# Zero products, one product piece per unit and other spacing in the forward loop of a training-step kernel

## The chip, the cores and the metric

The kernel runs on one core of a Trainium2 chip. The metric is the time of one execution on the device in microseconds (us): the median of seven runs, with the lowest and the highest. Beside these there is one execution taken with the hardware profiler. Its own time is given too, because all durations below come from it.

A core has five engines that run side by side: TensorE (PE: matmuls, and PEld: their weight loads), VectorE (DVE), ScalarE (ACT), GpSimd (POOL) and SyncE (SP, which here only issues DMAs). TensorE writes its results into PSUM, which has eight banks of 128 x 512 float32.

## The reference

It is one transformer block with adaptive layer norm, forward and backward, on 2048 tokens of width 512. There are 32 attention heads of 16 columns and a hidden layer of 1792. Weights and activations are bfloat16.

```python
sa, ca, ga, sb, cb, gb = split(silu(c) @ w_mod, 6)
h = layernorm(x) * (1 + ca) + sa
q, k, v = heads(h @ wqkv)
x = x + ga * (softmax(q @ k.T * 16 ** -0.5) @ v) @ wo
h = layernorm(x) * (1 + cb) + sb
z = relu(h @ w1 + b1)
x = x + gb * ((z * z) @ w2 + b2)
# returned: x and the gradients of x, wqkv, wo, w1, b1, w2, b2, c and w_mod for grad_out
```

## The kernel before, in words

The kernel has three parts: a preparation, a forward loop, and everything after it (the last dense chunk, the backward pass of the attention, the last products). The change is in the forward loop. It also adds one memset to the preparation.

The forward loop has 512 units (`NF`): four chunks of 512 queries, in each chunk eight groups of four heads, in each group 16 tiles of 128 keys (`TT`). A unit `u` does this, and the order in which it is written here is the order on each engine, since the whole loop is built with a manual schedule:

- `run_due`: DMAs and other small jobs that an earlier unit put off with `later(lag, ...)`.
- In units with `u % 16 == 4` (10 in the first seven groups), `fload`: nine DMAs on SP for the heads that come twelve or more units later.
- `fscore(u)`: four score matmuls in two pairs. A pair is 32 rows by 128 columns of the array each, side by side in different row strips, into one tile `psST` of two banks; there are three such tiles. ScalarE takes the exponential of a pair from `psST` to `ET` (line 555).
- `fpv(u - 2)`: four matmuls of 128 rows by 32 columns, side by side in column strips, add exponentials times values to the bank `oacc` (line 569). After the 16th key tile, which is in the units with `u % 16 == 1`, VectorE copies `oacc` to `ostage` (line 573). There is one `oacc` bank, so the next group's first `fpv` waits for this copy.
- The planned products of the preparation in units 0 to 100 (`plan`): projections, norms, and transposes `ptk` (line 1056).
- `step(u)`: one step of the dense work, described next. In units 101 to 143, and at other times, there is none.

The six `psST` banks and the `oacc` bank leave one bank for all products: the tile `pm`, which `mm()` gives out with one buffer. A product waits until VectorE has read the one before it from `pm`.

The dense work for a query chunk is a generator, `dense_chunk`. It is begun when that chunk's attention is done: chunk 0 near unit 136, chunk 1 near 264, chunk 2 near 392. Chunk 3 is done after the loop. `step` resumes the generator once for each unit, and what it yields is the number of units to wait. A yield of -2 makes `step` run a weight-gradient chain in the same unit (`next_chain`: four matmuls on line 228, and a copy of the result on line 246). Ripe chains also take units of their own. The stages are, in order:

- four pieces with `wo` (line 342), each followed on VectorE by a copy, two elementwise operations and a layer-norm statistic (lines 343, 324, 325, 329, 330);
- 14 products with `w1` (line 393);
- 14 products `dz` with the transposed `w2` (line 407). After every third one, chains are forced until few enough stand in the queue `dwq`, and then the result goes to `to_tokens`, which transposes it by a DMA and queues new chains;
- four `dx` products of 14 matmuls each (line 429), spread over four units, with a layer-norm gradient on VectorE (`finish_dx`, lines 456 to 461). The last `finish_dx` is run when the generator is resumed after the last product;
- four products with `w2` (line 480) from the weight tile `wB`, which SP loads in seven slices, and four with the transposed `wo` (line 512).

`open_group[0]` tells that a product which is spread over several units still holds the `pm` bank.

Of the kernel before, what the change touches and what calls it, by code (L numbers as in the profile page):

```python
# [17 lines left out]
BF = dt.bfloat16  # L18
# [16 lines left out]
def kernel(  # L35
# [29 lines left out]
    masks.make_identity(nc, identf[:])  # L65
    ones_bf = persist.tile([P, P], BF, name="ones_bf")
    DVE.memset(ones_bf[:], 1.0)
    onesf = persist.tile([P, 4], F32, name="onesf")
    DVE.memset(onesf[:], 1.0)
    modbc = persist.tile([P, 6, D], BF, name="modbc")  # L70
# [74 lines left out]
    with ExitStack() as ph:  # L145
# [6 lines left out]
        racc = ffw.tile([P, 5, D], F32, name="racc")  # L152
        pools = {}

        def mm():
            return pools["mm"].tile([P, 512], F32, name="pm", tag="pm")

        def flat(x):
# [156 lines left out]
        def dense_chunk(c, O_c, L):  # L315
# [23 lines left out]
            for ti in range(4):  # L339
                pa = mm()  # L340
                for oc in range(DC):
                    PE.matmul(pa[:], OT[:, ti, oc, :], L["wo"][:, oc, :], start=(oc == 0), stop=(oc == DC - 1))
                DVE.tensor_copy(a_c[:, ti, :], pa[:])
                with_input(ti)
                stats(ti)
                yield 0
            woT = ffw.tile([P, DC, D], BF, name="woT", tag="wo")
            later(3, sp, woT[:], woT_st[:])
            h2T = cb.tile([P, 4, DC, P], BF, name="h2T", tag="T4")
# [54 lines left out]
            for fc in range(FC):  # L404
                pds = mm()
                for oc in range(DC):
                    PE.matmul(pds[:], w2T[:, oc, fc * P:(fc + 1) * P], gfT[:, :, oc, :],
                              start=(oc == 0), stop=(oc == DC - 1))
                db1p = wk.tile([P, 1], F32, name="db1p", tag="db1p")
                DVE.scalar_tensor_tensor(out=dzT[:, fc, :], in0=pds[:], scalar=2.0, in1=rT[:, fc, :],  # L410
                                         op0=ALU.mult, op1=ALU.mult, accum_out=db1p[:])
                POOL.tensor_tensor(db1acc[:, fc:fc + 1], db1acc[:, fc:fc + 1], db1p[:], ALU.add)
                if fc % 3 == 2 or fc == FC - 1:
                    f0 = fc // 3 * 3
                    while len(dwq) > FC - (fc + 1) + n_dz[0]:
                        yield -2
                    to_tokens("dz", dzT, f0, fc + 1)
                yield 0
            if c == QC - 2:
                begun["w1"] = load_wA(w1_src, 1)  # L420
            yield 1
# [3 lines left out]
            for ti in range(4):  # L425
                t = 4 * c + ti
                pdh = mm()
                for fc in range(FC):
                    PE.matmul(pdh[:], dzT[:, fc, ti * P:(ti + 1) * P], w1T[:, fc, :],
                              start=(fc == 0), stop=(fc == FC - 1))  # L430
                    if fc == 3 and rest:
                        rest.pop()()
                    if fc % 4 == 3:
                        open_group[0] = True
                        yield 0
                open_group[0] = False
                xn2 = xn2_c[:, ti, :]
                dxn2 = wk.tile([P, D], BF, name="dxn2", tag="dxn2")
                s1 = wk.tile([P, 1], F32, name="s1b", tag="s1b")
                DVE.tensor_tensor_reduce(out=dxn2[:], in0=pdh[:], in1=cb1_bc, scale=1.0, scalar=0.0,  # L440
                                         op0=ALU.mult, op1=ALU.add, accum_out=s1[:])
                prod2 = wk.tile([P, D], BF, name="prod2", tag="tc")
                s2 = wk.tile([P, 1], F32, name="s2b", tag="s2b")
                DVE.tensor_tensor_reduce(out=prod2[:], in0=dxn2[:], in1=xn2, scale=1.0, scalar=0.0,
                                         op0=ALU.mult, op1=ALU.add, accum_out=s2[:])
                rowsum(1, dxn2[:], t)
                rowsum(2, prod2[:], t)
                c12 = wk.tile([P, 2], F32, name="c12", tag="c12")
                DVE.tensor_scalar(c12[:, 0:1], s1[:], 1.0 / D, None, ALU.mult)
                DVE.tensor_scalar(c12[:, 1:2], s2[:], 1.0 / D, None, ALU.mult)  # L450
                tq = wk.tile([P, D], BF, name="tqb", tag="ta")
                DVE.tensor_scalar(tq[:], xn2, c12[:, 1:2], c12[:, 0:1], ALU.mult, ALU.add)

                def finish_dx(ti=ti, t=t, dxn2=dxn2, tq=tq):
                    uq = wk.tile([P, D], BF, name="uqb", tag="tb")
                    DVE.tensor_tensor(uq[:], dxn2[:], tq[:], ALU.subtract)
                    DVE.scalar_tensor_tensor(out=dx1_c[:, ti, :], in0=uq[:], scalar=rstd2[:, t:t + 1], in1=g_c[:, ti, :],
                                             op0=ALU.mult, op1=ALU.add)
                    proda = wk.tile([P, D], BF, name="proda", tag="tc")
                    DVE.tensor_tensor(proda[:], dx1_c[:, ti, :], a_c[:, ti, :], ALU.mult)  # L460
                    DVE.tensor_tensor(da_c[:, ti, :], dx1_c[:, ti, :], ga_bc, ALU.mult)
                    rowsum(3, proda[:], t)

                rest.append(finish_dx)
                yield 0
            rest.pop()()
            chains = [add_chain(c, 3, FC + 4 * NS + a, D, lambda ti, a=a: O_c[:, ti, a * P:(a + 1) * P], lambda ti: da_c[:, ti, :],
# [89 lines left out]
        def fpv(u):  # L557
            qc, hg, kt = funits[u]
            if kt == 0:
                fcur["o"] = pools["o"].tile([P, 512], F32, name="oacc", tag="oacc")  # L560
                if hg == 0:
                    fcur["rr"] = ework.tile([H, 512], F32, name="rrows", tag="rrows", bufs=1)
                    fcur["ou"] = ework.tile([P, 4, HG, P], BF, name="O_un", tag="O_un", bufs=1)
            oacc = fcur["o"]
            ET = fe.pop(u)
            for hq in range(4):
                h = hg * 4 + hq
                lhsT = vaug[:, kt].rearrange("p h c -> p (h c)")[:, h * (DH + 1):h * (DH + 1) + 32]
                PE.matmul(oacc[32 * hq:32 * hq + 32, :], lhsT, ET[:, hq, :],  # L569
                          start=(kt == 0), stop=(kt == TT - 1), tile_position=(0, 32 * hq), skip_group_check=True)  # L570
            if kt == TT - 1:
                ostage = ework.tile([P, 512], F32, name="ostage", tag="ostage", bufs=1)
                DVE.tensor_copy(ostage[:], oacc[:])  # L573
                obf = ework.tile([P, 512], BF, name="obf", tag="obf", bufs=2)
                if u == NF - 1:
                    fcur["last"] = ostage
                    return
                if hg == HG - 1:
                    DVE.tensor_copy(obf[:], ostage[:])
                else:  # L580
                    POOL.tensor_copy(obf[:], ostage[:])
                for hq in range(4):
                    h = hg * 4 + hq
                    later(2, sp, fcur["rr"][h:h + 1, :], ostage[32 * hq + 16:32 * hq + 17, :])
                later(3, sp, fcur["ou"][:, :, hg, :], obf[:], True)
                if hg == HG - 1:
                    fdone.append((u + 7, qc, fcur["rr"], fcur["ou"]))

        def scale_heads(O_c, ou, ti, t, g):
            DVE.tensor_tensor(O_c[:, ti, 0:64 * g].rearrange("p (g h d) -> p g h d", g=g, h=4),  # L590
# [111 lines left out]
        def turn_weights(i):  # L702
            if i == 2:
                turned["1"] = ffw.tile([P, FC, D], BF, name="w1T_0", tag="wB")
                turned["2"] = ffw.tile([P, DC, FF], BF, name="w2T_0", tag="wA")
                turned["o"] = ffw.tile([P, DC, D], BF, name="woT_0", tag="wo")
            if 2 <= i < 6:
                for fc in range(4 * (i - 2), min(FC, 4 * (i - 2) + 4)):
                    sp(turned["1"][:, fc, :], B_w1[:, fc * P:(fc + 1) * P], True)
            if 7 <= i < 11:  # L710
                sp(turned["2"][:, i - 7, :], B_w2[:, (i - 7) * P:(i - 6) * P], True)
                sp(turned["o"][:, i - 7, :], A_wo[:, (i - 7) * P:(i - 6) * P], True)
            if i == 12:
                sp(w1T_st[:], turned["1"][:])
                sp(w2T_st[:], turned["2"][:])
                sp(woT_st[:], turned["o"][:])
# [421 lines left out]
        with ExitStack() as ph2:  # L1138
# [3 lines left out]
            with tc.manual_schedule(engines={PE.engine, ACT.engine, DVE.engine, SP.engine, POOL.engine}):  # L1142
                fh[0, 0] = (qts[0], kts[0])
                for u in range(NF + 2):
# [9 lines left out]
                        later_stage(stages[u // 4])  # L1154
                    if u % 4 == 0 and 18 <= u // 4 < 32:
                        turn_weights(u // 4 - 18)
                    for f, args in plan.pop(u, ()):
                        f(*args)
                    if u < NF - 4:
                        step(u)  # L1160
                    elif dwq and u >= NF - 2:
                        next_chain()
                    if u >= NF - 7 and "L" in loads and "O" not in loads["L"]:
                        early_finish()
                    if u == NF:
# [853 lines left out]
```

## Time and profile before

| | |
|---|---|
| seven runs | median 2582.5 us, 2578.74 to 2585.96 |
| the profiled execution | 2594.22 us, span 2592.2 us |
| mean granted TensorE clock | 0.910 |
| the forward loop in it | about 41 to 1037 us |
| behind the loop | 1037 to 2592.2 us |
| PE / DVE / ACT / POOL busy over the span | 91% / 70% / 89% / 13% |

In the page's groups, a row gives line, engine, operation, what it writes and reads, the count, the busy time, the mean of one in ns, and the idle time of the engine just before these instructions with what ended it. In tables by stretch, a row is a stretch (from:to in us from the start of the span), then the busy time of each engine with its number of instructions, the granted TensorE clock (1.00 is full speed) and the share of the DMA engines. In a timeline, a row is the start, the duration, the engine, the line and the operation, how many were merged, and in brackets the engine's idle time before the row with what ended it. Matmuls overlap in the pipeline and their ends are modelled, so a busy PE is not PE at its peak.

### The profile page before, as it was taken

The numbers are of one execution on the slowest core, as the hardware profiler recorded it, in microseconds if no ns is written. First come the engines' busy times: TensorE is split into PE (matmuls) and PEld (weight loads), VectorE is DVE, ScalarE is ACT, GpSimd is POOL, SyncE is SP. The second block draws the span as 40 slices with busy tenths as digits, with TensorE's granted clock in tenths as the row PEclk, the third lists the DMA queues.
The fourth block names the chain that finished last, engine by engine and source line by source line (L and its number), as shares of the span: only waits on it lengthen the run. The fifth ranks groups of instructions, "written<-read, shape, count | busy, mean of one in ns | idle before, by whom it ended". The sixth has DMA issues, their size and how long they took to land.

```text
span 2592.2 us, 49491 instructions
## 1 busy us (share of the span) xinstructions
PE 2355.8 (91%) x18468; PEld 761.3 (29%) x18468; DVE 1812.9 (70%) x2316; ACT 2312.3 (89%) x3577; POOL 348.1 (13%) x370
## 2 busy tenths in 40 slices
PE   7888999889988989999999999999899999999999
PEld 3232123222322322432222222222222222222243
DVE  5555253454444444578999989899898998999862
ACT  7999999999989999539999999999999999999943
POOL 2000101211323132210101101011010110100100
PEclk9995589989988999998999989999998998999999
DMA  6476563357548656979999999999999999999972
GB/s 202 127 195 170 145 154 95 90 156 152 81 94 179 124 118 126 259 214 187 198 189 198 188 197 196 190 194 191 196 196 195 205 195 195 196 197 207 191 240 76
DMA packets 1227126, 447.15 MB, mean 172 GB/s; under 512 B 1103095, under 2 KB 1197751, under 8 KB 1226630
## 3 DMA queue, kind: packets, MB, share of 16 engines
q1 hardware_dynamic: 1198966, 409.14, 79.6%
q0 software_dynamic: 10944, 16.78, 4.6%
q10 hardware_dynamic: 16976, 18.07, 2.5%
q8 instruction: 145, 2.38, 0.4%
q14 instruction: 95, 0.78, 0.1%
HBM read 96.75 MB, written 73.95 MB: 66 GB/s over the span
## 4 chain that ended last, share of the span: by engine, by line
PE 48%; ACT 34%; DVE 7%; issue 6%; DMA 2%; SPq 1%; ACTq 0%; POOL 0%; DVEq 0%; POOLq 0%
ACT E_u L1585 20%; ACT ET L555 9%; PE dqacc L1657 6%; PE psST L553 5%; PE psS_A L1579 4%; PE accVK L1630 3%; ACT dsT L1728 3%; PE oacc L569 3%; PE psS_C L1579 3%; PE pm L228 3%; PE psS_B L1579 2%; PE pm L393 2%; PE accVK L1639 2%; PE pdh L1843 2%; PE pwq L1877 2%
## 5 line engine op out<-in xcount | busy, mean ns | idle before, releaser
L1599 DVE TENSOR_TENSOR dS_u<-psD_u,E_u 128x1024 bf16<-128x1024 f32 x1024 | 1187.5, 1220 | 115.6 <-PE psS_B L1579 69.0
L555 ACT ACTIVATE ET<-psST 128x1024 bf16<-128x1024 f32 x1024 | 945.9, 1190 | 54.1 <-PE psST L553 53.5
L1585 ACT ACTIVATE E_u<-psS_A 128x512 bf16<-128x512 f32 x768 | 507.3, 661 | 26.7 <-PE psS_B L1579 9.6
L1585 ACT ACTIVATE E_u<-psS_B 128x512 bf16<-128x512 f32 x768 | 503.6, 656 | 6.2 <-PE ptT L1620 2.3
L1597 PE MATMUL psD_u<-iv,ido 32*128 32x512 bf16 x2048 | 429.7, 403 | 0.2
L553 PE MATMUL psST<-qt_sb,kt_sb 32*128 32x512 bf16 x2048 | 353.0, 431 | 55.3 <-ACT ET L555 42.7
L1585 ACT ACTIVATE E_u<-psS_C 128x512 bf16<-128x512 f32 x512 | 334.2, 653 | 1.1 <-PE accVK L1639 0.7
L1579 PE MATMUL psS_B<-ik,iq 32*128 32x512 bf16 x768 | 311.5, 406 | 12.7 <-ACT E_u L1585 5.2
L1579 PE MATMUL psS_A<-ik,iq 32*128 32x512 bf16 x768 | 309.7, 403 | 12.7 <-ACT E_u L1585 1.3
L569 PE MATMUL oacc<-ET,vaug 128*32 128x512 bf16 x2048 | 230.6, 440 | 7.0 <-DVE ostage L573 7.0
L1630 PE MATMUL accVK<-dS_u,qz 128*32 128x512 bf16 x2048 | 230.1, 418 | 0.3 <-DVE dS_u L1599 0.2
L1579 PE MATMUL psS_C<-ik,iq 32*128 32x512 bf16 x512 | 194.9, 381 | 33.0 <-ACT dsT L1728 29.0
L1579 PEld LDWEIGHTS <-iq 32*128 32x128 bf16 x2048 | 129.1, 92 | 313.7 <-issue 298.5
L1639 PE MATMUL accVK<-E_u,dOs_tok 128*16 128x512 bf16 x2048 | 208.7, 397 | 0.0
L1675 POOL TENSOR_TENSOR dQacc<-dQacc,dqtmp 128x512 f32<-128x512 f32 x64 | 81.2, 1268 | 885.3 <-ACT dqtmp L1670 885.3
L1657 PE MATMUL dqacc<-dsT,KS_tok 128*32 128x512 bf16 x2048 | 189.6, 482 | 11.2 <-DMA dsT<-dS_u 2.2
L553 PEld LDWEIGHTS <-kt_sb 32*128 32x128 bf16 x2048 | 87.2, 93 | 345.8 <-issue 327.5
L246 DVE COPY part<-pm 128x512 f32<-128x512 f32 (+2 forms) x103 | 63.5, 617 | 134.9 <-PE pm L228 132.5
L1728 ACT ACTIVATE dsT<-ptT 128x1024 bf16<-128x1024 bf16 x128 | 149.0, 1164 | 2.9 <-PE ptT L1620 2.7
L1597 PEld LDWEIGHTS <-ido 32*128 32x128 bf16 x2048 | 107.3, 91 | 109.1 <-issue 105.3
L1630 PEld LDWEIGHTS <-qz 128*32 128x32 bf16 x2048 | 61.4, 99 | 243.4 <-issue 230.8
L1620 PE MATMUL ptT<-identb,dS_u 128*128 128x128 bf16 x1024 | 79.2, 221 | 33.0 <-ACT dsT L1728 26.3
(400 smaller groups left out, 2309.8 us busy)
## 6 DMA issues: line engine op xcount, KB each, us to landing
p_st<-part POOLq DMA_DIRECT2D x36, 256.0 KB, 5.4
kt_sb<-qkT_st SPq DMA_DIRECT2D x124, 64.0 KB
wA<-in_B_w_dram SPq DMA_DIRECT2D x28, 256.0 KB
dsT<-dS_u SPq DMA_TRANSPOSE x448
wB<-w1T_st SPq DMA_DIRECT2D x21, 256.0 KB
wA<-w2T_st SPq DMA_DIRECT2D x21, 256.0 KB
wB<-in_B_w_dram SPq DMA_DIRECT2D x21, 256.0 KB
p_st<-part POOLq DMA_DIRECT2D x25, 192.0 KB, 4.3
```

The lines of the kernel that those rows point to most:

```text
L553: PE.matmul(ps[:, hi, :], kt_sb[r:r + 32, kt * P:(kt + 1) * P], qt_sb[r:r + 32, :], start=True, stop=True, tile_position=(r, 0))
L555: ACT.activation(ET[:, 2 * pair:2 * pair + 2, :], ps[:], AF.Exp, scale=SCALE)
L569: PE.matmul(oacc[32 * hq:32 * hq + 32, :], lhsT, ET[:, hq, :], start=(kt == 0), stop=(kt == TT - 1), tile_position=(0, 32 * hq), skip_grou ...
L1579: PE.matmul(psS[:], st["q"][r:r + 32, qt * P:(qt + 1) * P], st["k"][r:r + 32, kc * 512:kc * 512 + 512], start=True, stop=True, tile_positi ...
L1585: ACT.activation(bst[u][0][:, hq, :], sst.pop((u, hq))[:], AF.Exp, scale=SCALE)
L1597: PE.matmul(psD[:, hi, :], st["do"][r:r + 32, qt * P:(qt + 1) * P], st["v"][r:r + 32, kc * 512:kc * 512 + 512], start=True, stop=True, til ...
L1599: DVE.tensor_tensor(dS_u[:, 2 * pair:2 * pair + 2, :], psD[:], E_u[:, 2 * pair:2 * pair + 2, :], ALU.mult)
L1630: PE.matmul(cur["vk"][32 * hq:32 * hq + 32, :], hst[hg]["qz"][:, qt, hq, :], bst[u][1][:, hq, :], start=(qt == 0), stop=False, tile_positi ...
L1639: PE.matmul(acc[32 * hq:32 * hq + DH, :], dOs_tok[:, qt, (hg * 4 + hq) * DH:(hg * 4 + hq + 1) * DH], E_u[:, hq, :], start=False, stop=(qt ...
L1657: PE.matmul(acc[32 * hq:32 * hq + 32, :], KS_tok[:, kc * 4 + kt, h * DH:h * DH + 32], tT[:, :, hq * 4 + kt, :], start=(kt == 0), stop=(kt ...
L1675: POOL.tensor_tensor(dst2, dst, tmp[:], ALU.add)
L1728: ACT.activation(dst, pt[:], AF.Identity)
```

## The change

It has four parts, all in the forward loop.

- A tile of zeros, 128 x 16, is set once. `steady(u - 2)` adds two matmuls with these zeros as weights to `oacc`, so the values there stay what they are. It is called at the end of a unit in which `mm()` was not called and no spread product holds `pm`, and not in a unit whose `fpv` was the 16th key tile. This is the case in 133 units.
- In the `dz` stage, the `yield 0` after each product stands before the forced chains and `to_tokens`, and no longer behind them.
- The `wo` pieces of chunks 0 and 1 yield 1 instead of 0 after the first three pieces.
- Before the last `finish_dx` there is one more `yield 0` if the unit is divisible by 16.

```diff
+    zeros = persist.tile([P, DH], BF, name="zeros")
+    DVE.memset(zeros[:], 0.0)
...
+        products = [0]
+
         def mm():
+            products[0] += 1
             return pools["mm"].tile([P, 512], F32, name="pm", tag="pm")
...
                 with_input(ti)
                 stats(ti)
-                yield 0
+                yield int(c < QC - 2 and ti < 3)
...
                 POOL.tensor_tensor(db1acc[:, fc:fc + 1], db1acc[:, fc:fc + 1], db1p[:], ALU.add)
+                yield 0
                 if fc % 3 == 2 or fc == FC - 1:
                     f0 = fc // 3 * 3
                     while len(dwq) > FC - (fc + 1) + n_dz[0]:
                         yield -2
                     to_tokens("dz", dzT, f0, fc + 1)
-                yield 0
...
                 rest.append(finish_dx)
                 yield 0
+            if unit[0] % TT == 0:
+                yield 0
             rest.pop()()
...
+        def steady(u):
+            if 0 <= u < NF and funits[u][2] < TT - 1:
+                for _ in range(2):
+                    PE.matmul(fcur["o"][0:DH, :], zeros[:], identb.unsqueeze(1).to_broadcast([P, 4, P]), start=False, stop=False,
+                              tile_position=(0, 0), skip_group_check=True)
...
+                    count, begun_group = products[0], open_group[0]
                     for f, args in plan.pop(u, ()):
                         f(*args)
                     if u < NF - 4:
                         step(u)
                     elif dwq and u >= NF - 2:
                         next_chain()
+                    if products[0] == count and not (begun_group or open_group[0]):
+                        steady(u - 2)
```

## The prediction

> **What bounds the kernel now.** I read the page first, then ScalarE's and TensorE's timeline through the forward loop, then tables of busy time by stretch.
>
> ```profile
> PEclk9995589989988999998999989999998998999999
> ...
> L555 ACT ACTIVATE ET<-psST 128x1024 bf16<-128x1024 f32 x1024 | 945.9, 1190 | 54.1 <-PE psST L553 53.5
> ...
> L553 PE MATMUL psST<-qt_sb,kt_sb 32*128 32x512 bf16 x2048 | 353.0, 431 | 55.3 <-ACT ET L555 42.7
> ```
>
> The forward loop has 512 units, each with two exponentials on ScalarE. They are 945.9 us busy, 1.85 us a unit (steady units start 1.83 apart), between 41 and 1037 us. Their idle time, 54.1 us, is all that the loop can lose, and nearly all of it ends with late scores (psST). So I sum only that idle time: work that another engine gains or loses counts where it makes a psST late. In the steady state TensorE waits for ScalarE instead (42.7).
>
> ```profile
> core 0: us, PE busy (x) PEld busy (x) DVE busy (x) ACT busy (x) POOL busy (x), PEclk, DMA share, GB/s
> 236.80:299.00 62.20, 57.60 (x276) 10.80 (x272) 12.10 (x11) 62.20 (x70) 0.62 (x1) 0.50 0.52 144
> 344.00:371.00 27.00, 24.74 (x172) 8.28 (x168) 16.41 (x28) 26.13 (x30) 0.61 (x1) 0.95 0.48 95
> ...
> 134.81:138.22 3.41, 2.91 (x23) 0.89 (x21) 2.46 (x5) 3.41 (x5) 0.61 (x1) 1.00 0.41 159
> 138.22:141.63 3.41, 3.41 (x26) 1.12 (x24) 1.84 (x3) 3.41 (x5) 0.00 (x0) 1.00 1.05 255
> 148.46:151.88 3.42, 2.50 (x24) 0.93 (x20) 1.58 (x4) 3.42 (x5) 0.00 (x0) 1.00 1.04 277
> 151.88:155.29 3.41, 3.41 (x18) 0.76 (x16) 0.69 (x1) 2.63 (x4) 0.00 (x0) 0.50 0.91 245
> ```
>
> Units without a product (first row) run at clock 0.50 and ScalarE still never idles: half clock alone costs nothing. What costs is the first product after such a stretch, and a stall, for which PE at half speed has no reserve. Four such stalls:
>
> ```profile
> 391.10 1.02 PE L228 MATMUL pm<-gf_c,tk 128*128 128x512 bf16 x4 [0.86 <-DVE rT L410]
> ...
> 392.55 2.85 ACT L555 ACTIVATE ET<-psST 128x1024 bf16<-128x1024 f32 x3 [1.42 <-PE psST L553]
> ```
> ```profile
> 572.81 1.02 PE L342 MATMUL pm<-wo_nat,OT 128*128 128x512 bf16 x4 [2.61 <-DVE a_c L343]
> ...
> 574.26 3.77 ACT L555 ACTIVATE ET<-psST 128x1024 bf16<-128x1024 f32 x4 [2.35 <-PE psST L553]
> ```
> ```profile
> 470.63 1.26 DVE L456 TENSOR_TENSOR uqb<-dxn,tqb 128x512 bf16<-128x512 bf16 x1
> ...
> 474.32 0.62 PE L569 MATMUL oacc<-ET,vaug 128*32 128x512 bf16 x4 [1.83 <-DVE ostage L573]
> ```
> ```profile
> 741.85 0.59 PE L480 MATMUL pm<-wB,sT 128*128 128x512 bf16 x2 [3.02 <-DMA wB<-in_B_w_dram]
> ```
>
> In order: two products in one unit, the second waiting for the only pm bank; wo pieces coming faster than VectorE works them off; the oacc bank waiting for its copy, which stands behind the last dx step on VectorE; a weight slice that SP issued late.
>
> **The change part by part.** Units below are those of the loop; chunk 0, 1, 2 are the dense chunks. The built order of the changed kernel gives the places.
>
> *One product per unit in dz.* The yield now stands before the forced weight-gradient chain. Eight units held two products (3.77 us for 1.83). ScalarE's idle after them: 1.42, 1.37, 1.42, 1.37, 1.45, 1.40, 1.40, 1.34 = 11.2 us. The extra units replace product-free units of the same stage (the loop's unit count is fixed), so they cost nothing. The tk transposes on SP and the chains, with their p_st stores and POOL's accumulating DMAs, come up to a few units later; chunk 2's products are in the same units again from 458 on, so nothing spills behind the loop. Gain 11.2.
>
> *wo pieces every second unit,* chunks 0 and 1 only. One piece is 0.69 + 0.42 + 0.42 + 0.69 + 0.18 = 2.4 us of VectorE, more where POOL's sums run (L324 takes 1.37 instead of 0.42), against 1.83 us of a unit, now 3.67. Idle at the pieces, the clock's share apart: 0.18 + 0.68 + 0.79 and 1.01 + 2.35 = 5.0 us. The oacc copy at unit 145 still queues behind the first piece's 2.4 us and the empty unit after it covers that; I take 4.5. Chunk 2 keeps its 1.0 + 3.4.
>
> *The last dx step.* Its test is on a unit divisible by 16. In the new order that step resumes in units 227, 355 and 475, none divisible: the edit itself never fires. But chunks 0 and 1 now run three units later, so the step comes after the oacc copy (units 225, 353) instead of ahead of it: the two stalls of 0.78 go, 1.6 us. The three units also move the wB slices against SP's nine head loads (units 228, 356): the last slice, issued at 737.88 behind them and needed at once, is now due after them and needed five units later. Its idle, 2.69 + 1.42 + 0.81 and 0.42 in chunk 0, is 5.3. I take 6 of the 6.9. h2T, daT and the w2T slices move three units likewise, with waits of five units written around them: nothing.
>
> *Zero products.* 133 units without another product get two 128x16 matmuls into oacc, after that unit's own. At full clock a 512-column matmul takes (1.02 - 0.38) / 3 = 0.21 us, so 0.43 us, into PE's idle 0.72 us of such a unit: free, and the next psST has it behind it. No new wait; the memset lies before the first input. What it is worth is the clock. The clock changes only on a grid of 3.41 us. In each window I summed matmul time weighted by the share of the array: psST counts a quarter each (two of four row strips at once), oacc a quarter (four column strips at once), products one. Below about 0.38 of the window the next one is at half; at half clock it takes over about 0.75 to return. A product-free unit has 0.43 / 1.83 = 0.23; with a product 0.70. 148.46 has 0.34 and is followed by 0.50.
>
> Does a lone 128x16 count one or a quarter? The Trainium skill's page "TensorE: Matmul & The Clock Gate", section "Part 3: Packing small matmuls", says a tile occupies its own strips, so a quarter: 0.29, clock down. But 134.81 holds five lone 128x32 norm matmuls (L797): by strips 0.33, yet the clock stays. They must count over 0.4 each; a matmul over all 128 rows counting as one gives 0.52. I take one: 0.47 per zero unit, which holds the clock, and at half clock (0.43 + 0.43 + 0.85) / 2.06 = 0.83 brings it back. The same page's closing table ("Why this matters for your kernels") asks only for no PE gap over about 3 us; by that, the first row above should be warm (57.6 of 62.2 us busy) and the zeros are worth nothing, leaving 22 us in all. The row shows 0.50, so the measurement decides.
>
> Restarts from half clock that would go: 0.92, 0.87, 1.20, 0.85, 0.95, 1.31, 0.92, 0.95, 0.50, 1.07, 0.78, 0.23 and some 0.7 of the end = 11.2. I take 10, and charge 1.5 for windows that still fall cold (the unit in 16 without zeros, VectorE's three stalls near 200 to 226 us), where a zero unit is PE's 2.06 us.
>
> Sum: 11.2 + 4.5 + 6 + 10 - 1.5 = 30 us off the profiled 2594.2, so 2564. That execution is 12 us above the median of the seven runs, and its 3 us DMA stall may be rarer there, so I subtract 28.5 from 2582.5: **2554**. What lies behind the loop (1555 us) keeps its instructions. It has its own half-clock windows, whose phase moves by 30 us: I allow 4 us either way, which also takes in the runs' spread (2578.7 to 2586.0).
>
> **Rivals.**
> - *The zeros count a quarter (slower).* At half clock a product unit measured 2.92 us (474.87 to 477.79); less two of its four 0.43 us matmuls, a zero unit is 2.06, PE-bound, 0.23 over ScalarE. About 80 zero units in cold stretches cost 18; 16 with four transposes besides (0.43 more) cost 10.6. 29 lost against 22 gained: +7, about 2589. It decides where a lone 128x16 counts below 0.6: the stretches around 240 to 300 us then stay at 0.50. For: the strips rule. Against: 134.81. 0.17.
> - *The idle comes back elsewhere.* PE in alternating transpose and product units (52 to 66) comes to about 3.6 of 3.67 us with the zeros, and a shifted copy or load meets another burst. Half the gain: 2568. For: 3 units of shift gave both the oacc and the wB stall their places. 0.13.
> - The forecast: 0.70.
>
> **How the numbers follow.** A measurement here tells about 0.2% (5 us) from no change: 2577.3 to 2587.7. The forecast's own range is 2543 to 2566; to 2584 it takes in the second rival and the lower part of the first. Faster: 0.70 + 0.10 of the rivals = 0.80; same 0.07; slower 0.13, the rest of the first rival.
>
> **What would show it.** ET's idle falls from 54 to about 22 us with its busy time unchanged; PEclk is near 1.0 from 237 to 344 us; no unit with two products; the waits of L228 for the pm bank after L410 gone; the oacc wait near 474 and 723 gone; chunk 2's wo pieces still idle 3 to 4 us. Wrong if PEclk stays at 0.50 there and zero units start 2.06 us apart, or if new ET idle appears at wo pieces or heads' first units.

## The result, and the profile after

The changed kernel takes 2560.27 us (median of 12 runs, 2550.35 to 2568.96). Beside it on the same chip the kernel before took 2581.27 us (31 runs, 2572.45 to 2588.75). The ratio is 0.9916 with a 95% interval of 0.9903 to 0.993: 21.7 us faster, between 18 and 25. The profiled execution took 2560.86 us, its span 2559.0 us, at a mean clock of 0.955.

The page of the changed kernel, with the same three lines that were shown of before (ScalarE's exponentials are now L562, the scores L560):

```profile
PEclk9999999999999999999999999999999999999999
...
L562 ACT ACTIVATE ET<-psST 128x1024 bf16<-128x1024 f32 x1024 | 943.0, 1245 | 32.3 <-PE psST L560 31.5
...
L560 PE MATMUL psST<-qt_sb,kt_sb 32*128 32x512 bf16 x2048 | 315.7, 388 | 50.4 <-ACT ET L562 46.0
```

No slice of the span is below nine tenths of full clock any more: of the time from 41 us to the end of the loop, 242 us were at half clock before and 48 are now. The exponentials are busy for 943.0 us, within 3 us of before, and their idle time fell from 54.1 to 32.3 us. That is 21.8 us, about what the comparison measured, though part of the agreement is luck (see below). The table by stretch has the same columns as before:

```profile
core 0: us, PE busy (x) PEld busy (x) DVE busy (x) ACT busy (x) POOL busy (x), PEclk, DMA share, GB/s
232.00:299.00 67.00, 55.79 (x368) 14.18 (x366) 12.44 (x12) 67.00 (x74) 0.62 (x1) 0.92 0.51 139
...
340.00:367.00 27.00, 24.60 (x173) 8.41 (x172) 13.93 (x24) 27.00 (x30) 0.61 (x1) 1.00 0.62 115
```

Units without a product ran at clock 0.50 before and run at 0.92 now. In the `w1` stage after them ScalarE does not idle at all (27.00 of 27.00 us; before 26.13).

The four stalls of the prediction, in the timeline of the changed kernel. A double unit of `dz` has become two units, and the chain (L233, formerly L228) has no wait in brackets. ScalarE runs through 17 exponentials without a gap:

```profile
377.49 15.76 ACT L562 ACTIVATE ET<-psST 128x1024 bf16<-128x1024 f32 x17
...
385.82 1.02 PE L233 MATMUL pm<-gf_c,tk 128*128 128x512 bf16 x4
...
387.62 1.02 PE L412 MATMUL pm<-gfT,wA 128*128 128x512 bf16 x4
```

At the last dx step the copy of `oacc` now comes ahead of that step on VectorE, and `oacc<-ET,vaug` follows it without a wait:

```profile
462.83 0.69 DVE L580 COPY ostage<-oacc 128x512 f32<-128x512 f32 x1 [2.87 <-PE oacc L576]
...
464.21 0.40 PE L576 MATMUL oacc<-ET,vaug 128*32 128x512 bf16 x4
...
466.52 0.91 DVE L461 TENSOR_TENSOR uqb<-dxn,tqb 128x512 bf16<-128x512 bf16 x1
```

At chunk 1's `wo` pieces one gap remains. The copy of `oacc` stands behind the first piece's work on VectorE, TensorE waits 0.93 us, and the next scores come 1.69 us late (2.35 before, with others beside it):

```profile
559.12 0.62 PE L576 MATMUL oacc<-ET,vaug 128*32 128x512 bf16 x4 [0.93 <-DVE ostage L580]
559.67 1.89 PE L347 MATMUL pm<-wo_nat,OT 128*128 128x512 bf16 x4
562.20 3.77 ACT L562 ACTIVATE ET<-psST 128x1024 bf16<-128x1024 f32 x4 [1.69 <-PE psST L560]
```

The fourth stall, a slice of `wB` that comes late, has not gone. It was 3.02 us of TensorE's time and is now 6.18:

```profile
718.40 5.13 SPq L178 DMA_TRANSPOSE daT<-a_c  x1
723.58 3.81 SPq L178 DMA_DIRECT2D wB<-in_B_w_dram  x4
730.46 1.01 PE L487 MATMUL pm<-wB,sT 128*128 128x512 bf16 x2 [6.18 <-DMA wB<-in_B_w_dram]
732.12 1.94 ACT L562 ACTIVATE ET<-psST 128x1024 bf16<-128x1024 f32 x2 [6.39 <-PE psST L560]
```

The idle time of the exponentials by place, summed from the trace over the units of each stage, in us:

| place | before | after |
|---|---|---|
| `dz`, chunks 0, 1, 2 | 11.2 | 0.3 |
| `wo`, chunks 0, 1 | 6.8 | 2.1 |
| `w1`, last dx step and the units after it, all chunks | 8.4 | 0.0 |
| `w2` (the `wB` slices), chunks 0, 1 | 5.3 | 10.5 |
| `wo`, chunk 2 | 5.4 | 6.1 |
| begin of chunk 1 (units 263 to 271) | 1.3 | 2.4 |
| VectorE's stalls, units 81 to 100 | 4.0 | 4.2 |
| units 0 to 6 | 5.9 | 3.5 |
| the rest | 5.8 | 3.0 |
| sum | 54.1 | 32.3 |

Single places differ between executions. Units 0 to 6 lie before anything that the change moves; they gave 3.5 us in some runs and up to 6.1 in others, with and without the change. So 2.4 of the 21.8 us are not the change's. The begin of chunk 1 gave 0.2 to 1.7 us in before and the four experiments with at most one of the `dz` and `wo` parts, and 1.7 to 5.6 in the nine profiles with both. So the wait there grew a little. It is not new: the chains' stores `p_st` stand on SP behind the head loads in both kernels. Before, VectorE waited 2.43 us for one to free its buffer; now it waits 3.26, and TensorE 2.64 for VectorE. The first of these lines is of before:

```profile
547.73 0.42 DVE L246 COPY part<-pm 128x256 f32<-128x256 f32 x1 [2.43 <-DMA p_st<-part]
```
```profile
538.19 1.86 SPq L178 DMA_DIRECT2D p_st<-part  x4
...
540.32 0.56 DVE L251 COPY part<-pm 128x384 f32<-128x384 f32 x1 [3.26 <-DMA p_st<-part]
...
540.93 0.30 PE L658 MATMUL pm<-identf,rrows 32*128 32x32 f32 x2 [2.64 <-DVE part L251]
...
541.68 1.94 ACT L562 ACTIVATE ET<-psST 128x1024 bf16<-128x1024 f32 x2 [2.16 <-PE psST L560]
```

Behind the loop the two profiled executions took 1554.2 us (before) and 1544.5 us (after). Over all runs with a profile this part was 1537 to 1556 us long, in no relation to the parts of the change (1537.2 with the `wo` part alone, 1556.4 with the zeros alone). The two profiled executions differ by 33 us, some 12 more than the comparison, and 9.7 us of that lie behind the loop. So the loop's idle time is the better measure.

### The profile page after: what moved, and what is told of

The parts are those of the page before. It is cut to its first block, busy times and chain, and to the rows that moved or that the text cites. A ratio compares the mean times of both kernels' runs of the same rounds, so it can differ in the third digit from the quotient of the medians.

```text
span 2559.0 us, 50017 instructions
## 1 busy us (share of the span) xinstructions
PE 2330.7 (91%) x18734; PEld 765.6 (30%) x18734; DVE 1810.9 (71%) x2317; ACT 2307.6 (90%) x3577; POOL 347.9 (14%) x370
## 4 chain that ended last, share of the span: by engine, by line
PE 45%; ACT 36%; DVE 7%; issue 7%; DMA 3%; SPq 1%; ACTq 0%; DVEq 0%; POOL 0%; POOLq 0%
ACT E_u L1601 21%; ACT ET L562 11%; PE dqacc L1673 6%; PE psS_A L1595 4%; PE psST L560 4%; ACT dsT L1744 3%; PE accVK L1646 3%; PE pm L233 3%; PE psS_C L1595 2%; PE psS_B L1595 2%; PE oacc L576 2%; PE accVK L1655 2%; PE pdh L1859 2%; PE pwq L1893 2%; PE pm L487 2%
## 5 line engine op out<-in xcount | busy, mean ns | idle before, releaser
L562 ACT ACTIVATE ET<-psST 128x1024 bf16<-128x1024 f32 x1024 | 943.0, 1245 | 32.3 <-PE psST L560 31.5
L1613 PE MATMUL psD_u<-iv,ido 32*128 32x512 bf16 x2048 | 423.8, 398 | 1.8 <-DVE dS_u L1615 1.4
L560 PE MATMUL psST<-qt_sb,kt_sb 32*128 32x512 bf16 x2048 | 315.7, 388 | 50.4 <-ACT ET L562 46.0
L1595 PE MATMUL psS_B<-ik,iq 32*128 32x512 bf16 x768 | 305.6, 398 | 11.2 <-ACT E_u L1601 3.7
L1595 PE MATMUL psS_A<-ik,iq 32*128 32x512 bf16 x768 | 304.3, 396 | 12.5 <-ACT E_u L1601 1.3
L576 PE MATMUL oacc<-ET,vaug 128*32 128x512 bf16 x2048 | 208.4, 397 | 1.9 <-DVE ostage L580 1.9
L1673 PE MATMUL dqacc<-dsT,KS_tok 128*32 128x512 bf16 x2048 | 182.3, 465 | 15.0 <-DMA dsT<-dS_u 2.9
L560 PEld LDWEIGHTS <-kt_sb 32*128 32x128 bf16 x2048 | 85.1, 91 | 341.3 <-issue 320.4
L1636 PE MATMUL ptT<-identb,dS_u 128*128 128x128 bf16 x1024 | 79.2, 221 | 33.1 <-ACT dsT L1744 26.3
```

The source lines that it names most:

```text
L560: PE.matmul(ps[:, hi, :], kt_sb[r:r + 32, kt * P:(kt + 1) * P], qt_sb[r:r + 32, :], start=True, stop=True, tile_position=(r, 0))
L562: ACT.activation(ET[:, 2 * pair:2 * pair + 2, :], ps[:], AF.Exp, scale=SCALE)
L1595: PE.matmul(psS[:], st["q"][r:r + 32, qt * P:(qt + 1) * P], st["k"][r:r + 32, kc * 512:kc * 512 + 512], start=True, stop=True, tile_positi ...
L1613: PE.matmul(psD[:, hi, :], st["do"][r:r + 32, qt * P:(qt + 1) * P], st["v"][r:r + 32, kc * 512:kc * 512 + 512], start=True, stop=True, til ...
L1673: PE.matmul(acc[32 * hq:32 * hq + 32, :], KS_tok[:, kc * 4 + kt, h * DH:h * DH + 32], tT[:, :, hq * 4 + kt, :], start=(kt == 0), stop=(kt ...
```

## The experiments

All ratios are to the kernel before, run on the same chip between the kernel's own runs, with a 95% interval. "Idle" is the exponentials' idle time in the profiled execution, which is one execution of each kernel. "Cold" and "warm" mean TensorE at half and at full granted clock; a "restart" is the idle time of ScalarE at the first product after a cold stretch.

**Which part brings what**

*The change without the zero products.*

```diff
-                    if products[0] == count and not (begun_group or open_group[0]):
-                        steady(u - 2)
```

> The change without its zero products, all else as in it. Theory (the zeros keep the clock up, and half clock costs at the first product after it): the exponentials' idle time rises from 32 us of the changed kernel to 40 to 44, the clock is back at 0.50 between about 235 and 300 us, and the time is some 9 us above the changed kernel: 0.995 of before. Rival (the spacing of the products did it all, the clock costs nothing since ScalarE sets the pace): idle stays at 32, 0.9915 of before.

Measured: 2571.9 us, 0.9949 (0.9932 to 0.9967), idle 43.3. The row by stretch:

```profile
236.00:299.00 63.00, 58.26 (x274) 10.84 (x275) 11.18 (x9) 63.00 (x71) 0.61 (x1) 0.50 0.50 141
```

The clock is back at 0.50 with TensorE busy for 58.26 of 63.00 us, and 11.0 us of idle time return, most of them in the `wo` and `w1` stages, after the last dx step and at the end: the prediction's restarts. So the zeros are worth 8.5 us in the comparison (0.9949 against 0.9916); with both intervals, some 3 to 14.

*The zero products alone* (the other three parts undone).

> Before with the zero products alone. Theory: the restarts from half clock go (some 10 us of idle), the eight double products, the wo pieces, the oacc wait and the wB wait stay: idle 54 to about 43, 0.996 of before. Rival (once the clock is up the engine only reaches the same waits earlier, so zeros help only together with the spacing): idle above 50, 0.999 of before.

Measured: 2571.26 us, 0.9965 (0.9952 to 0.9979), idle 40.9:

```profile
236.00:299.00 63.00, 52.20 (x344) 13.29 (x343) 9.30 (x6) 63.00 (x69) 0.61 (x1) 0.92 0.49 141
```

That is 9.0 us. Here `dz` keeps its double units (2.79 us in chunk 0), but the `wB` stall of chunk 1 fell from 4.92 to 0.80 us. SP issued the last slice 3.17 us after the first `w2` product began instead of 4.20, and TensorE had it 3.1 us after its issue instead of 4.0. That the warm clock is behind this was not shown; in the `dz` part alone, which is cold, the stall stayed at 4.8.

*The `dz` part alone*: the kernel before with its `yield 0` moved ahead of the chains.

> Before with the moved yield in dz alone. Theory: the idle of 11.2 us after the eight double products goes and nothing else moves in chunk 2: idle 43, 0.9955 of before. Rival (the late products come back as waits in the following dx stage or at the end of the loop): idle 48 or more, 0.998 or above.

Measured: 2570.47 us, 0.9957 (0.9944 to 0.997), idle 39.7, with 0.0 us left in the `dz` stages. That is 11.1 us. With the 9.0 us of the zeros alone it makes 20.1 of the 21.7 us of the whole change.

*The `wo` spacing alone.*

```diff
-                yield 0
+                yield int(c < QC - 2 and ti < 3)
```

> Before with the spaced wo pieces of chunks 0 and 1 alone. Theory: their idle falls from 6.8 to about 3.5 us and the oacc wait behind the last dx step goes (1.6), both chunks now running three units later; but the same three units put the wB slices behind the head loads and daT on SP, and that wait grows from 5.3 to about 10 us. Sum near nothing: idle 53 to 55, 0.999 of before. Rival (the longer wB wait comes from the dz edit or from the zeros): wB stays at 5.3, idle 49, 0.9975.

Measured: 2581.65 us, 0.9997 (0.9983 to 1.0011), idle 51.2. The pieces of chunks 0 and 1 idle 5.4 instead of 6.8 us, and chunk 1's `w2` stage 7.1 instead of 4.9: what is won at the pieces is lost at the slices. TensorE is cold here and `dz` is as before, so this growth comes from the three units alone. Chunk 0's `w2` stage has none (0.0 instead of 0.4 us).

*The extra yield before the last dx step alone.*

> Before with the extra yield ahead of the last dx step alone; here it does fire, at units 224 and 352. Theory: the oacc wait goes and the idle after it falls from 4.1 to about 2 us (the restart from half clock stays), the wB slices move by one unit; idle about 51, 0.9985 to 1.000 of before, not to be told from no change.

Measured: 2577.71 us, 0.999 (0.9975 to 1.0006), idle 48.8. In the order of the kernel before, the step does fall on units divisible by 16, so the yield fires; the units after it idle 2.5 instead of 4.1 us in chunks 0 and 1. The comparison can't tell this from nothing.

*The changed kernel without that yield.* The yield never fires in the changed kernel, so this is the changed kernel once more.

```diff
-            if unit[0] % TT == 0:
-                yield 0
```

> The changed kernel without the extra yield ahead of the last dx step. Its instructions stand in the same order on all five engines as the changed kernel's. Theory (the edit never fires there): 0.9916 of before, as the changed kernel. There is no rival but the spread of the runs.

Measured: 2561.25 us, 0.9911 (0.9882 to 0.9939), idle 35.1, of which 8.6 us in chunk 1's `w2`. In the full change this part is text without effect. The 2.8 us between 35.1 and 32.3 also shows how far two profiled executions of one program lie apart.

**What holds the clock**

Three versions of the zero products, everything else as in the changed kernel. They tell a rule by strips from a rule by rows, and both from "TensorE is busy".

```diff
-                for _ in range(2):
+                for _ in range(1):
```

> The changed kernel with one zero matmul in a unit instead of two. Theory (a lone matmul over 128 rows counts as one while it streams, and a window needs about 0.38): a zero unit counts 0.23 + 0.12 = 0.35, too little, so the stretch from 237 to 299 us is at 0.50 as without zeros, and the time is near that, 0.995 of before. Rival (any activity without a long gap holds the clock): 1.00 there and 0.9915.

```diff
-                for _ in range(2):
-                    PE.matmul(fcur["o"][0:DH, :], zeros[:], ..., tile_position=(0, 0), ...)
+                for j in (0, 32):
+                    PE.matmul(fcur["o"][j:j + DH, :], zeros[:], ..., tile_position=(0, j), ...)
```

> The changed kernel with its two zero matmuls side by side, in the column strips at 0 and at 32 of the array, instead of one after the other in one strip. Theory (what counts is the time in which rows stream, however many column strips do so at once): 0.23 + 0.12 = 0.35, the clock falls, 0.50 from 237 to 299 us. Rival (each matmul counts by itself, one each): 0.47, clock 1.00 there. By strips, a quarter each: 0.29, 0.50.

```diff
-                    PE.matmul(fcur["o"][0:DH, :], zeros[:], identb.unsqueeze(1).to_broadcast([P, 4, P]), ...)
+                    PE.matmul(fcur["o"][:, :], identb[0:32, :], zeros[0:32, :].unsqueeze(1).to_broadcast([32, 32, DH]), ...)
```

> The changed kernel with zero matmuls of 32 rows by 128 columns, identity as weights and zeros streamed, two in a row in the first row strip; the same two times 0.21 us on the engine. Theory (rows count): each counts a quarter, 0.29 for a zero unit, so 0.50 from 237 to 299 us and near 0.995 of before. Rival (a lone matmul counts one whatever its shape, busy time is what counts): 1.00 there and 0.9915.

Measured: one zero product 2572.28 us, 0.996 (0.9938 to 0.9983); two side by side in two column strips 2571.27 us, 0.9958 (0.9944 to 0.9972); two of 32 rows and 128 columns 2585.97 us, 1.003 (1.0017 to 1.0043). The row by stretch of each, in this order:

```profile
236.00:299.00 63.00, 61.56 (x311) 11.10 (x309) 9.20 (x6) 63.00 (x70) 0.71 (x2) 0.52 0.49 147
```
```profile
236.00:299.00 63.00, 60.66 (x340) 11.18 (x337) 10.54 (x7) 63.00 (x70) 0.62 (x1) 0.54 0.48 137
```
```profile
236.00:299.00 63.00, 62.82 (x332) 16.07 (x328) 13.25 (x14) 61.35 (x64) 0.61 (x1) 0.50 0.50 143
```

All three are cold, and in all three TensorE is busier than in the changed kernel, whose clock is 0.92 in this stretch with 52.16 us busy. With the prediction's count (a matmul over all 128 rows counts one, alone or side by side; fewer rows count in proportion), a zero unit has 0.35 of the window with one product or with two at once, and 0.29 with the row tiles. Two after another give 0.47. The bound that the prediction read from before, 0.38, separates them.

The same count holds far beyond these stretches. It was worked out for every window of 3.41 us between 45 and 1000 us in all fourteen traces (512 columns take 0.21 us at full clock and 0.43 at half). Of the windows at full clock, all 147 below 0.35 were followed by half clock, and none of the 3081 above 0.40. Of those at half clock, none of the 326 below 0.67 were followed by full clock, and all 159 above 0.76 were. A count by strips in both directions, rows and columns, places 96 and 55 windows wrongly at its best bounds; the count by rows places 13 and 8 wrongly. The two bounds also tell why one zero product fails: it cannot bring the clock back either (0.55 to 0.73 in the half-clock windows of its stretch, where the changed kernel's cold windows reach 0.90 and 0.88).

One zero product, and two side by side, keep what the rest of the change brings (0.9949 without zeros) and gain nothing measurable from their zeros. Their idle is 33.1 and 42.1 us. The 33.1 comes from an execution of 2564.39 us, 8 us below the median of that kernel, so the comparison is taken and not this one profile.

The row tiles are the prediction's first rival come true: zeros that cost TensorE time and do not hold the clock. In TensorE's timeline of that kernel, units with transposes start 2.48 us apart and pure zero units 1.93 (238.12, 240.59, 243.07, 245.00):

```profile
238.12 0.62 PE L576 MATMUL oacc<-ET,vaug 128*32 128x512 bf16 x4
...
240.59 0.62 PE L576 MATMUL oacc<-ET,vaug 128*32 128x512 bf16 x4
...
243.07 0.62 PE L576 MATMUL oacc<-ET,vaug 128*32 128x512 bf16 x4
243.62 0.60 PE L599 MATMUL oacc<-zeros,identb 32*128 32x512 bf16 x1
...
245.00 0.62 PE L576 MATMUL oacc<-ET,vaug 128*32 128x512 bf16 x4
```

Idle is 52.5 us, of which 11.0 in units 81 to 100, and against the change without zeros the ratio is 0.8% worse.

**The `wB` slices**

The theory: SP's queue order holds the slices back. In before, three slices were issued ahead of the transpose `daT`, three behind it (the sixth among the lines left out here), and only the seventh behind the nine head loads:

```profile
716.83 1.43 SPq L173 DMA_DIRECT2D wB<-in_B_w_dram  x3
...
722.63 2.14 SPq L173 DMA_TRANSPOSE daT<-a_c  x1
724.82 1.51 SPq L173 DMA_DIRECT2D wB<-in_B_w_dram  x2
...
737.88 0.43 SPq L173 DMA_DIRECT2D wB<-in_B_w_dram  x1
```

In the changed kernel two slices are issued, then the nine head loads, then one slice, then the store `dx_st` and `daT`, and only then the last four. SP issues without a pause of over 0.2 us from 706.2 to 727.4 us:

```profile
710.98 1.07 SPq L178 DMA_DIRECT2D wB<-in_B_w_dram  x2
712.09 2.17 SPq L140 DMA_DIRECT2D kt_sb<-qkT_st  x4
714.30 2.32 SPq L140 DMA_DIRECT2D qt_sb<-qkT_st  x4
716.71 0.55 SPq L140 DMA_DIRECT2D qt_sb<-m_st  x1
717.31 0.44 SPq L178 DMA_DIRECT2D wB<-in_B_w_dram  x1
717.85 0.45 SPq L178 DMA_DIRECT2D dx_st<-dx_c  x1
718.40 5.13 SPq L178 DMA_TRANSPOSE daT<-a_c  x1
723.58 3.81 SPq L178 DMA_DIRECT2D wB<-in_B_w_dram  x4
```

The rivals were that the slices' own transfers are slow, whenever they are issued, or that what is won here is lost at the next burst. The experiment puts off all seven slices by one unit, instead of one to five, and so issues them ahead of the head loads:

```diff
-            w2_nat = load_wB(w2_src, 1, 0.67)
+            w2_nat = load_wB(w2_src, 1, 0)
```

> The changed kernel with all seven wB slices queued on SP in the first unit after the last dx step, so ahead of the nine head loads and of the daT transpose. Theory (the slices are late because of their place in SP's queue): the waits of 6.2 and 1.5 us for wB go, the idle falls from 32 to about 22 us, 0.9875 of before. Rival (the DMA engines are full there, a slice lands no earlier whatever its place, or the head loads and daT become late instead): idle stays near 32, 0.9915.

> The changed kernel with early wB slices once more, now on one chip with the changed kernel's instructions (the run above). Theory: 0.988 of before, about 9 us under the changed kernel, since the wait for wB is gone. Rival (the first measurement fell on a fast chip): the same as the run above.

Measured: 2546.35 us, 0.9878 (0.9852 to 0.9904), idle 24.6; and on another chip 2548.99 us, 0.9864 (0.9838 to 0.9891), idle 21.1, beside 2561.25 us of the changed kernel (without its silent yield) on that chip. SP's queue and the page of the first:

```profile
709.62 3.94 SPq L178 DMA_DIRECT2D wB<-in_B_w_dram  x7
713.61 2.07 SPq L140 DMA_DIRECT2D kt_sb<-qkT_st  x4
...
721.05 6.56 SPq L178 DMA_TRANSPOSE daT<-a_c  x1
```
```profile
L562 ACT ACTIVATE ET<-psST 128x1024 bf16<-128x1024 f32 x1024 | 942.6, 1250 | 24.6 <-PE psST L560 23.9
```

The slices are out at 713.6, the `w2` stages idle 0.0 us in chunk 1 and at most 0.04 in chunk 0 in both runs, and nothing takes their place, though `daT` now holds SP for 6.56 us: nobody waits for it yet. So an early issue is enough. Whether the head loads or `daT` cost the slices more was not separated, since the experiment puts them ahead of both. This version beats both kernels, the changed one by 12.3 us on the chip where both ran.

*The same, with the `wo` spacing in chunk 2 too.* Three of the chains no longer fit into the loop here and are run behind it, too late for the gradient of w1, which is not whole in this version.

```diff
-                yield int(c < QC - 2 and ti < 3)
+                yield int(c < QC - 1 and ti < 3)
```

> The changed kernel with the wB slices early, and the wo pieces of chunk 2 spread over every second unit as well. Theory (chunk 2 has idle units behind its wo pieces to give away): the idle of 6.4 us at its wo pieces falls to about 2.5, the time to 0.9865 of before. Rival (chunk 2 ends three units later, and what is left of its chains is done after the loop, where nothing hides it): the gain at the pieces is given back, 0.988 or above.

Measured: 2555.42 us, 0.9907 (0.9885 to 0.9928), idle 24.7. Chunk 2's pieces have 4.4 us of idle time, against 6.4 and 4.2 in the two profiles without the spacing, so a gain there can't be told from the spread. The sum is no lower (24.6 and 21.1 without it), and the time is no better than without it, probably worse (0.9878 and 0.9864 there): the loop is no shorter, and three chains more are left for the time behind it. That part took 1554.8 us in the profiled execution against 1545.4, which is within its spread, so why it is longer was not separated.

What remains in chunk 2 is not VectorE's rate alone. In the changed kernel the first piece waits for its operand, a transpose that was issued 11.8 us earlier, behind nine head loads and three others and ahead of six `wA` loads:

```profile
791.18 4.65 SPq L178 DMA_TRANSPOSE OT<-O_c  x1
795.88 8.07 SPq L178 DMA_DIRECT2D wA<-in_B_w_dram  x6
```
```profile
803.00 1.89 PE L347 MATMUL pm<-wo_nat,OT 128*128 128x512 bf16 x4 [2.26 <-DMA OT<-O_c]
```

Moving those loads was not tried. SP issued nothing for 4.3 us ahead of this transpose, and in the repeat with the early slices the first piece does not idle ScalarE at all, so what makes it late in some executions stays open.

## Why the prediction was right, and where it was wrong

It said faster, by 28.5 us to 2554 us; measured were 21.7 us, 2560.3 us. Direction, mechanism and range held. One step of the sum failed, and its size is larger than the whole miss. That the total came so near has luck in it: 2.4 us of the measured gain in idle time lie in units 0 to 6, which the change does not touch.

- **One product per unit in `dz`: right.** 11.2 forecast; the stage's idle time fell by 10.9, and this part alone measured 11.1 us. The moved chains cost nothing.
- **The zeros and the clock: right.** 10 less 1.5 forecast; 11.0 us of idle time between the versions with and without them, 8.5 us in the comparison, 9.0 us alone. A lone 128x16 product counts as one. The rule by strips, which the prediction derived from the strips of a tile in the Trainium skill's page "TensorE: Matmul & The Clock Gate", section "Part 3: Packing small matmuls", would have had the zeros fail. The clock of 0.92 decides against it for products that run alone. The prediction's allowance for cold windows was hardly needed: in the changed kernel the clock still dips after units 113 and 129, which get no zeros, but ScalarE idles 0.00 us there, and VectorE's stalls cost 4.2 us where they cost 4.0 before.
- **The `wo` spacing: most of it.** 4.5 us forecast at the pieces, and some 1.8 of restarts there; 4.6 came in all. The prediction saw the copy of `oacc` queue behind the first piece's work and let the empty unit cover it. In chunk 0 that is so (0.45 us left); in chunk 1 it is not (0.93 us of TensorE, 1.69 of ScalarE).
- **The last dx step: right on both counts.** The edit does not fire (the kernel without it has its stages in the same units and takes the same time), and the shift by three units took the two `oacc` waits of 0.78 us away; the exponentials idle 0.00 us there.
- **The `wB` slices: wrong.** This is the term that failed: "is now due after them and needed five units later. Its idle ... is 5.3. I take 6 of the 6.9." Instead of falling from 5.3 to near 0, it rose to 10.5. The prediction looked at the one slice that was late before (the last one, behind the head loads) and found it five units of room. Its text does not lay out the whole SP queue in the new order, in which the head loads stand ahead of five slices instead of one, and ahead of `daT`, which is itself ahead of the last four. Its line that `h2T`, `daT` and the `w2T` slices "move three units likewise ... nothing" takes no account of `daT`'s time on SP either: 2.14 us before and 5.13 now. That time is not the shift's alone, though: without the shift, `daT` took 4.34 us in the `dz` part alone. That the shift is behind chunk 1's loss shows across the runs. Chunk 1's `w2` idles 7.0 to 8.6 us in six of the seven runs with the three units of shift and late slices (4.6 in the seventh, the zeros side by side), warm or cold, and 0.8 to 4.9 us in the four without the shift. For chunk 0 (0.4 before, 2.4 now) it is not shown: its `w2` idles 2.5 us in the `dz` part alone, without the shift, and 0.0 with it in the `wo` part alone. That early issue is enough in both chunks, and that the transfers themselves are not too slow, shows in the version with early slices: at most 0.04 us.
- **Chunk 2's `wo` pieces: as said in part.** 3 to 4 us of VectorE's were to stay; 6.1 us stayed. Of these, 3.2 are at the later pieces and 2.8 at the first one, where TensorE waits 2.26 us for the late transpose, which the prediction did not have.

The second rival, that idle time comes back elsewhere by the shift, was thus partly true, at the place that the prediction had counted as a gain. With the slices early, the change is worth 31 to 35 us (0.9878 and 0.9864), a little above the sum of 30. The first rival did not occur in this change, but its price was near what another kind of zeros costs: forecast were 2.06 us for a cold zero unit, 2.49 with transposes, and 2589 us; the row tiles measured 1.93, 2.48 and 2585.97. The row tiles differ in how they overlap with the scores, so this is not a test of that rival's sum.

## What to carry to other kernels

When a change moves a stage by a few units, write out the whole DMA queue in its new order before and after the move, with each issue's duration (with a margin, since `daT`'s was 2.14 to 6.56 us here) and the unit in which its data are needed. Looking only at the transfer that is late now will miss the ones that the move puts behind something else. And where an engine with reserve is slowed by its clock only between bursts, a little filler can be worth nearly as much as the best real edit (9.0 us alone against 11.1 here), but only if it is of a kind that the clock counts: try one piece, two side by side and two in turn, and read the granted clock, not the busy time.

## What the runs showed of the hardware that was not expected

- TensorE at 0.98 busy (61.56 of 63.00 us) ran at clock 0.52, and at 0.83 busy (52.16 of 63.00 us) at 0.92. At half clock everything takes longer, so a busy row is a sign of the cold state here, not of work that would end it.
- Two 128x16 products at once in two column strips did not hold the clock (0.54) where the same two in turn did (0.92). Two of 32 rows by 128 columns in turn did not (0.50).
- One and the same transpose by DMA (`daT`, chunk 1) held SP for 2.14 us in before, 5.13 in the changed kernel, and 6.56 and 5.68 in the two profiles with early slices. The loads ahead of it in SP's queue do not explain this alone: in the `dz` part alone the same four issues stood ahead of it at the same distances as in before, and it took 4.34 us. What sets the time stays open.
- A count of matmul time, weighted by the share of the array's rows in use and with products that run at once counted as one, fits the granted clock: bounds near 0.38 (down) and 0.74 (up) over windows of 3.41 us misplace 21 of 3903 windows in the fourteen traces.
